# Seven products instead of four double ones in two more pairs, two sets of accumulators, and a new order of work, in an attention and two-MLP kernel

## The chip, the cores and the metric

The kernel runs on one core of one Trainium2 chip. The metric is the device time of one execution in microseconds (us), the median of several runs.

## What is computed

```python
scores = scale * np.matmul(q, k.transpose(0, 1, 3, 2))          # q, k, v: 4 x 8 x 576 x 64
thresh = np.max(scores, axis=-1, keepdims=True) - tau
scores = np.where(scores >= thresh, scores, -1000000000.0)
attn = np.exp(scores - np.max(scores, axis=-1, keepdims=True))
attn = attn / (np.sum(attn, axis=-1, keepdims=True) + 1e-09)
x = np.matmul(attn, v)                                           # as 2304 tokens x 512
h = x @ w_in1                                                    # 512 x 2048
x = (np.maximum(h, 0.0) + alpha * np.minimum(h, 0.0)) @ w_out1   # 2048 x 512
h = x @ w_in2
out = (h - np.tanh(h)) @ w_out2
```

The four weight matrices arrive as 64-bit floats and are made into 32-bit ones on the chip.

## The kernel before

The 2304 tokens are taken in 9 blocks of 256, and each MLP goes through them as blocks 0 to 8 (first MLP) and 9 to 17 (second). Most products are done in split form: an operand is kept as a rounded high part and the remainder (low part), and one product is three matmuls, low with high, high with high, high with low.

**Order of the work.** Nothing loops at run time. Every step is given to `Plan.add` with the engines that may do it, a cost for each, a rank and what it reads and writes; `Plan.order` then simulates the engines and issues, on the engine that can begin first, the ready step with the lowest rank. The constants above the class (`PA`, `OFF`, `POOL_PEN` and so on) are the ranks and penalties. So a change of ranks moves steps on all engines, and can give a copy or a subtraction to another engine. TensorE has 140 filler steps of two matmuls (line 1211) with the last rank, done where nothing else is ready; attention, the first MLP and the preparation of weights run interleaved until attention ends.

**Second MLP.** The 2048 hidden rows of a block are 8 pairs of 2 x 128. For pair n of block m:
- `h_pair` (line 961): 24 matmuls of 256 columns into one PSUM bank. In the second MLP they go to `hp` and to `pt` by turns (line 965), each one bank. ScalarE then takes tanh from that bank (line 987) and VectorE subtracts it (line 994) into `mr`. Only after that may the bank be written again.
- `g` is made from `mr`. With Strassen's algorithm (`STRASSEN`, line 37: pairs 0, 2, 3, 4, 5, 6) VectorE forms four sums `gs` of 128 columns (line 1033), and the seven 128-column operands are split into high and low parts in two pieces (384 and 512 columns).
- `out_products` (line 1069): a Strassen pair adds seven products of 256 columns, 21 matmuls, into seven half banks of `sc` (line 1084). Pairs 1 and 7 are plain: four products of 512 columns, 12 matmuls, into two banks (line 1091).
- After pair 7 the sums of the half banks are formed on VectorE (line 1117) and stored. There is one set of accumulators, the four banks of `sc`, which attention used before.

`out_pair` (line 398) prepares a pair's weights: two loads, `rebias`, `three`, `ends_` and `middle` to make 32-bit floats, and for a Strassen pair four differences (line 430), copies to high parts and subtractions to low parts (line 290). `home` says whose memory it takes: weights of the first MLP that are done with, or what attention leaves.

On TensorE the order in the second MLP is, with few exceptions, the 24 matmuls of one pair, then the output products of the pair before it.

Of the kernel before, what the change touches and what calls it, by code (L numbers as in the profile page):

```python
# [22 lines left out]
P = 128  # L23
BLK = 256
# [23 lines left out]
POOL_PEN = 0.3611  # L50
ACT_PEN = 0.1795
# [6 lines left out]
XR = 18.318  # L58
# [18 lines left out]
class Plan:  # L77
# [38 lines left out]
    def order(self):  # L116
# [42 lines left out]
        late_pen = {"ACT": 0.1, "DVE": 0.0, "POOL": 0.8}  # L159
# [74 lines left out]
def attention_mlp_mlp(ctx: ExitStack, tc: tile.TileContext, kv, q0, q1, tau, w1i, w1o, alpha, w2i, w2o, out):  # L234
# [84 lines left out]
    def turned_float(l, kind, qd, c, rank):  # L319
# [45 lines left out]
        add(any_of(0.56, 0.59, 0.62), rank, three, reads=[raw], writes=[(*raw, 0)], late=l)  # L365
# [22 lines left out]

    def home(p):

        if p < 2:
# [3 lines left out]
        kind, qd = {2: ("o", 0), 4: ("o", 1), 6: ("o", 2), 3: ("i", 3), 5: ("o", 3)}[p]  # L395
        return (lambda: wpool), [f"{kind}{part}{qd}" for part in ("hi", "lo")], [f"{kind}{qd}"]

    def out_pair(p, rank):
# [33 lines left out]
        parts = []  # L432
        if strassen:
            for n_ in range(4):
                add({"DVE": 0.33, "POOL": 0.6}, rank, lambda e, n_=n_: combine(e, n_), reads=t + [(*tk[0], 0)] * (n_ == 1) + [(*tk[0], 1), (*tk[1], 0)] * (n_ == 3),
                    writes=[(*tk[n_ // 2], n_ % 2)], takes=[("o", tk[n_ // 2])] if n_ % 2 == 0 else [], late=True)
            parts = [(lambda: f(0, 0), 0, BLK, [t[0]]), (lambda: f(1), BLK, 3 * BLK, [t[1]]),
                     (lambda: T[tk[0]], 3 * BLK, 5 * BLK, [(*tk[0], 0), (*tk[0], 1)]),
                     (lambda: T[tk[1]], 5 * BLK, 7 * BLK, [(*tk[1], 0), (*tk[1], 1)])]
        else:  # L440
            parts = [(lambda: f(0), 0, 2 * BLK, [t[0]]), (lambda: f(1), 2 * BLK, 4 * BLK, [t[1]])]
        for n_, (x, a, b, r) in enumerate(parts):
            begins = [dst] + ([ROOM] if p < 2 else []) if n_ == 0 else []
            m = (b - a) / 512
            add(any_of(0.1 + 0.42 * m, 0.065 + 0.27 * m, 0.07 + 0.52 * m), rank, lambda e, x=x, a=a, b=b, n_=n_: hi(e, x, a, b, not n_),
                reads=r + ([dst] if n_ else []), writes=[(*dst, n_, 0), *begins], takes=[(x_, dst) for x_ in bufs] if n_ == 0 else [], late=True)
            add(either(0.06 + 0.54 * m, 0.05 + 1.18 * m), rank, lambda e, x=x, a=a, b=b: lo(e, x, a, b), reads=r + [(*dst, n_, 0)], writes=[(*dst, n_, 1)], late=True)
# [32 lines left out]
    def prep(v, rank):  # L480
# [133 lines left out]
    def softmax(tile, n, slots, rank):  # L614
# [346 lines left out]
    def h_pair(p, rank):  # L961
# [3 lines left out]
        hq = hps[l * (p % 2)]  # L965
        hpk, hb = ("hp", l * (p % 2)), [("hp", l * (p % 2))]
# [43 lines left out]
        if not l or p % NPAIR not in STRASSEN:  # L1010
# [55 lines left out]
    def two_banks(k):  # L1066
        return sc[k // 2][:, k % 2 * 512:(k % 2 + 1) * 512]

    def out_products(p, rank):
        m, n = p // NPAIR, p % NPAIR  # L1070
        w, g = ("wp", n), ("g", p)
        strassen = n in STRASSEN

        seven = [(0, 0, 1), (2, 1, 2), (1, 6, 4), (3, 3, 5), (4, 4, 6), (5, 5, 7), (6, 2, 3)]
        begun_banks = set()

        def emit_seven(e, now):
# [30 lines left out]
        def bank(number):  # L1108
            return half_bank(number)[0]
# [219 lines left out]
```

## Time and profile before

| | us |
|---|---|
| median of 3 runs | 1153.53 (1153.4 to 1154.03) |
| the profiled execution | 1156.25 |
| its span, first to last instruction | 1154.5 |
| TensorE busy | 1126.2, 98% of the span |
| VectorE busy | 919.6, 80% |
| ScalarE busy | 640.6, 55% |
| GpSimd busy | 214.4, 19% |

In the rows PE is TensorE's matmul side and PEld its weight loads, DVE is VectorE, ACT is ScalarE, POOL is GpSimd. The profile's times are from one execution. A row of the timeline merges neighbours of one kind: its length runs to the end of the last one, and since matmuls overlap, the distance between two starts is what a group costs. The VectorE rows overlap a little too, so the same holds there.

### The profile page before, as it was taken

Reading aid. Unit: us, or ns where it says so; the run is one execution under the profiler, and the core shown is the slowest. Engines: PE = TensorE matmul, PEld = TensorE weight load, DVE = VectorE, ACT = ScalarE, POOL = GpSimd, SP = SyncE. Lnnn points to the kernel's source line nnn. Section 1 sums busy time; section 2 is a strip of 40 time slices with the busy share of each in tenths; the row PEclk is TensorE's granted clock in tenths of the full one; section 3 lists DMA queues with packets and bytes.
Section 4 is the critical chain, followed back from the end, with each engine's and each line's share of the span. In section 5 each row is a group of like instructions: output and inputs, shape, how many; then the busy total and the mean of one; then the engine's idle time right before and its main releaser. Section 6 shows DMA issues by size and latency. Waiting matters only on the chain.

```text
span 1154.5 us, 23027 instructions
## 1 busy us (share of the span) xinstructions
PE 1126.2 (98%) x8889; PEld 1065.3 (92%) x8889; DVE 919.6 (80%) x2093; ACT 640.6 (55%) x1237; POOL 214.4 (19%) x215
## 2 busy tenths in 40 slices
PE   7999999999999999999999999998999999999998
PEld 6778877999999999999889999997999999999997
DVE  4998897999999998989999797999565565565554
ACT  4777776767667667667676554665223323322322
POOL 0333121232423413214223110010000000000000
PEclk9999999999999999999999999999999999999999
DMA  6654542312123202222112164441110010010000
GB/s 163 186 163 144 166 147 79 89 30 70 49 69 104 70 12 82 70 79 79 46 48 64 27 208 127 157 150 52 37 37 11 28 37 11 28 37 11 10 19 20
DMA packets 55822, 87.10 MB, mean 75 GB/s; under 512 B 18592, under 2 KB 33952, under 8 KB 55712
## 3 DMA queue, kind: packets, MB, share of 16 engines
q1 hardware_dynamic: 55712, 85.62, 24.5%
q8 instruction: 70, 1.15, 0.4%
q14 instruction: 40, 0.33, 0.1%
HBM read 75.64 MB, written 9.96 MB: 74 GB/s over the span
## 4 chain that ended last, share of the span: by engine, by line
PE 79%; DVE 12%; ACT 4%; DMA 2%; issue 2%; POOL 1%; SPq 0%; ACTq 0%; DVEq 0%; POOLq 0%
PE hp L975 21%; PE acc L1162 14%; PE sc L1084 10%; PE pt L975 8%; PE pt L691 4%; PE sc L1091 4%; PE sc L765 3%; PE sc L796 3%; PE acc L1211 2%; PE sc L788 2%; DVE eT L290 2%; DVE e L641 2%; PE sc L757 2%; PE sc L886 2%; DVE st L629 1%
## 5 line engine op out<-in xcount | busy, mean ns | idle before, releaser
L975 PE MATMUL hp<-x,ihi 128*128 128x256 f32 x1728 | 323.0, 285 | 0.5 <-DVE mr L996 0.5
L975 PEld LDWEIGHTS hp<-x,ihi 128*128 128x128 f32 x1728 | 265.3, 189 | 1.4 <-DVE mr L996 0.7
L975 PE MATMUL hp<-x,ilo 128*128 128x256 f32 x864 | 242.8, 281 | 0.0
L1162 PE MATMUL acc<-g,ohi 128*128 128x256 f32 x1152 | 217.2, 286 | 0.4 <-ACT o L285 0.4
L1162 PEld LDWEIGHTS acc<-g,ohi 128*128 128x128 f32 x1152 | 176.6, 189 | 1.4 <-issue 0.7
L975 PEld LDWEIGHTS hp<-x,ilo 128*128 128x128 f32 x864 | 162.9, 189 | 0.0
L1162 PE MATMUL acc<-g,olo 128*128 128x256 f32 x576 | 161.9, 281 | 0.0
L1084 PE MATMUL sc<-wp,g 128*128 128x256 f32 x1134 | 143.3, 280 | 3.9 <-DVE g L290 1.8
L1084 PEld LDWEIGHTS sc<-wp,g 128*128 128x128 f32 x1134 | 137.2, 188 | 5.3 <-DVE g L290 2.2
L641 DVE SCALAR_TENSOR_TENSOR e<-sc,st,e 128x576 f32<-128x576 f32 x144 | 115.4, 814 | 17.7 <-ACT e L637 8.3
L637 ACT ACTIVATE e<-sc,st 128x576 f32<-128x576 f32 x144 | 105.1, 740 | 26.7 <-DVE st L629 16.2
L629 DVE TENSOR_REDUCE st<-sc 128x1 f32<-128x576 f32 x144 | 105.6, 751 | 15.3 <-PE sc L757 8.1
L1162 PEld LDWEIGHTS acc<-g,olo 128*128 128x128 f32 x576 | 108.5, 188 | 0.0
L975 PE MATMUL pt<-x,ihi 128*128 128x256 f32 x576 | 104.1, 281 | 0.0
L285 ACT ACTIVATE eT<-pt 128x512 fp32r<-128x512 f32 (+1 forms) x144 | 85.6, 594 | 22.1 <-PE pt L691 19.9
L691 PE MATMUL pt<-ident,e 128*128 128x128 f32 x576 | 88.1, 275 | 8.6 <-ACT eT L285 4.0
L975 PEld LDWEIGHTS pt<-x,ihi 128*128 128x128 f32 x576 | 89.7, 189 | 1.4
L285 ACT ACTIVATE g<-mr 128x384 fp32r<-128x384 f32 (+1 forms) x98 | 56.3, 574 | 52.5 <-DVE mr L994 36.4
L975 PE MATMUL pt<-x,ilo 128*128 128x256 f32 x288 | 81.0, 281 | 0.0
L290 POOL TENSOR_TENSOR x<-rw,x 128x1024 fp32r<-128x1024 f32 x7 | 20.0, 2855 | 327.2 <-ACT x L285 236.7
L994 DVE TENSOR_TENSOR mr<-hp,mr 128x512 f32<-128x512 f32 x36 | 24.9, 692 | 68.9 <-ACT mr L987 68.9
L691 PEld LDWEIGHTS pt<-ident,e 128*128 128x128 f32 x576 | 65.4, 140 | 15.2 <-ACT eT L285 4.4
(127 smaller groups left out, 2091.7 us busy)
## 6 DMA issues: line engine op xcount, KB each, us to landing
rkv<-in_kv_dram SPq DMA_DIRECT2D x38, 288.0 KB, 2.8
rw<-in_w1i_dram SPq DMA_DIRECT2D x16, 512.0 KB, 4.6
rw<-in_w1o_dram SPq DMA_DIRECT2D x16, 512.0 KB, 4.3
rw<-in_w2i_dram SPq DMA_DIRECT2D x16, 512.0 KB, 4.3
rw<-in_w2o_dram SPq DMA_DIRECT2D x16, 512.0 KB, 4.4
rkv<-in_kv_dram SPq DMA_DIRECT2D x39, 160.0 KB, 2.9
ks<-in_kv_dram SPq DMA_DIRECT2D x18, 288.0 KB, 3.0
x1d<-o SPq DMA_DIRECT2D x18, 256.0 KB, 2.1
```

Source lines behind the costliest of these rows:

```text
L285: e.activation(out=out_, in_=in_, func=AF.Copy, **({} if scale is None else {"scale": scale}))
L290: e.tensor_tensor(out=out_, in0=in_, in1=hi.bitcast(F32), op=ALU.subtract)
L629: e.tensor_reduce(out=T[st][:, 0, j:j + 1], in_=x(s), axis=AX.X, op=ALU.max, negate=True)
L637: e.activation(out=weights(j), in_=x(s), func=AF.Exp, bias=T[st][:, 0, j:j + 1], scale=1.0)
L641: e.scalar_tensor_tensor(out=w_, in0=x(s), scalar=T[st][:, 1, j:j + 1], in1=w_, op0=ALU.is_ge, op1=ALU.mult, accum_out=T[st][:, 2, j:j + 1])
L691: e.transpose(pt[:, c, :], x[:, c * P:(c + 1) * P], ident)
L765: e.matmul(sc[j][:, 192:192 + S][:, c], lhsT=T["qs", v][:, part, j * P:(j + 1) * P], rhs=T["ks", k][:, (1 - j) * D:][:, c], start=(part == ...
L796: e.matmul(po, lhsT=vf[:, c], rhs=T[g][part][:, c, :], start=(c + part == 0), stop=False)
L975: e.matmul(hq[:, k, :], lhsT=weight(l, "i", part, f // 4)[:, c, (f % 4) * P:(f % 4 + 1) * P], rhs=T[f"x{x}", m][:, c, :], start=(n0 + n == ...
L1084: e.matmul(out_, lhsT=x[:, a], rhs=y[:, b], start=(n == 0 and i == 0 and number in (1, 2, 5, 4)), stop=(n == NPAIR - 1 and i == 2), skip_g ...
L1091: e.matmul(two_banks(3 - 2 * t), lhsT=x, rhs=y, start=False, stop=(n == NPAIR - 1 and k == 1 and i == 2), skip_group_check=True)
L1162: e.matmul(acc[t][:, (c % 2) * BLK:(c % 2 + 1) * BLK], lhsT=w[:, c * P:(c + 1) * P], rhs=g[:, k, :], start=(f == 0 and n == 0 and c % 2 == ...
```

## The change

It makes pairs 1 and 7 Strassen pairs. Their weights need 7 x 256 columns instead of 4 x 256, so `beside` puts the last pieces of pairs 6 and 7 into the free eighth of other pairs' tiles. Even and odd blocks get different accumulators: even ones `sc` as before, odd ones the two banks `acc`, the bank `pt` and, for product 4, the other half of `sc`'s last bank. So `h_pair` has only `hp`. Product 4 becomes a half-bank sum of its own at the block's end. Blocks 9 and 10 are taken side by side: pair 0 of both, pair 1 of both, and so on. The ranks, penalties and `RAW` (which scores are done unsplit) are new.

```diff
-STRASSEN = (0, 2, 3, 4, 5, 6)
-PA, PB = 272.298, 4.647
+PA, PB = 363.69, 1.658
-RAW = 20
+RAW = 18
-POOL_PEN = 0.3611
-ACT_PEN = 0.1795
+POOL_PEN = 0.2975
+ACT_PEN = 0
+LPOOL_PEN = 0.0058
+LACT_PEN = 0
...
-        late_pen = {"ACT": 0.1, "DVE": 0.0, "POOL": 0.8}
+        late_pen = {"ACT": LACT_PEN, "DVE": 0.0, "POOL": LPOOL_PEN}
...
+    def beside(p, b):
+
+        return ("wp", p if p < 6 or b < 4 else (b - 3 if p == 6 else b if b < 6 else 8))
...
-        hq = hps[l * (p % 2)]
-        hpk, hb = ("hp", l * (p % 2)), [("hp", l * (p % 2))]
+        hq, hpk, hb = hp, ("hp", 0), [("hp", 0)]
...
-        if not l or p % NPAIR not in STRASSEN:
+        if not l:
...
-    def half_bank(n):
-        k = {1: 0, 6: 1, 2: 2, 3: 3, 7: 4, 5: 5, 4: 6, 8: 7}[n]
-        return sc[k // 4][:, k % 4 * BLK:(k % 4 + 1) * BLK], k // 2
+    def bank_of(m, n):
+
+        if (m - NBLK) % 2 == 0 or n == 3:
+            return sc[n // 2][:, n % 2 * 512:(n % 2 + 1) * 512], ("c", n)
+        if n == 2:
+            return pt.rearrange("p c s -> p (c s)"), ("hp", 1)
+        return acc[n], ("acc", n)
+
+    def half_bank(m, n):
+        k = {1: 0, 6: 1, 2: 2, 3: 3, 7: 4, 5: 5, 4: 6 + (m - NBLK) % 2}[n]
+        x, key = bank_of(m, k // 2)
+        return x[:, k % 2 * BLK:(k % 2 + 1) * BLK], key
...
-        seven = [(0, 0, 1), (2, 1, 2), (1, 6, 4), (3, 3, 5), (4, 4, 6), (5, 5, 7), (6, 2, 3)]
+        seven = [(0, 0, 1), (4, 4, 6), (5, 5, 7), (3, 3, 5), (2, 1, 2), (6, 2, 3), (1, 6, 4)]
...
+        add({"DVE": 0.6}, r, lambda e: total(e, T[o[1]], bank_of(m, 1)[0], T[o[1]]), [keys[1], *oa, *ob], oa + ob, [keys[1]])
+        add({"DVE": 0.35}, r, lambda e: total(e, c(), bank(4), c()), [keys[3], *oc, *od], oc, [keys[3]])
...
+    first, two = NBLK * NPAIR, 2 * NPAIR
+    pairs = [*range(first), *(first + n // 2 + n % 2 * NPAIR for n in range(two)), *range(first + two, NP)]
```

What moves is shown at three places. The first is TensorE at the very end, where the output products of pair 7 of the last block begin (`wp` are weights, `g` values, `sc` the accumulators; x2 is two matmuls). Before, behind the last two products of pair 6:

```order
L1084 MATMUL sc_90<-wp_9841,g 128x256 x2
L1084 MATMUL sc_90<-wp_9842,g 128x256
L1084 MATMUL sc_89<-wp_9841,g 128x256 x2
L1084 MATMUL sc_89<-wp_9842,g 128x256
L1091 MATMUL sc_89<-wp_10200,g 128x512 x2
L1091 MATMUL sc_89<-wp_10201,g 128x512
```

Now, behind the first product of pair 7:

```order
L1101 MATMUL sc_89<-wp_10387,g 128x256 x2
L1101 MATMUL sc_89<-wp_10388,g 128x256
L1101 MATMUL sc_90<-tw,g 128x256 x3
L1101 MATMUL sc_89<-wp_9936,g 128x256 x2
L1101 MATMUL sc_89<-wp_9937,g 128x256
L1101 MATMUL sc_90<-wp_10075,g 128x256 x2
L1101 MATMUL sc_90<-wp_10076,g 128x256
L1101 MATMUL sc_90<-wp_10387,g 128x256 x2
L1101 MATMUL sc_90<-wp_10388,g 128x256
```

Twelve matmuls of 512 columns, of which the first three stand here, are now 21 of 256, some with weights that lie beside those of other pairs (`tw`, `wp_9936`, `wp_10075`).

The second is VectorE while the second MLP begins, the last rows ahead of the sixth subtraction of tanh (`mr`); `rw` and `tw` are weights being made into floats, `o` their differences, `wp` their low parts. Before:

```order
L290 TENSOR_TENSOR wp_10013<-o,wp_10012 128x512
L354 SCALAR_TENSOR_TENSOR rw<-rw 128x512
L290 TENSOR_TENSOR wp_10013<-o,wp_10012 128x512
L359 SCALAR_TENSOR_TENSOR tw<-tw,rw 128x512
L354 SCALAR_TENSOR_TENSOR rw<-rw 128x512 x2
L359 SCALAR_TENSOR_TENSOR tw<-tw,rw 128x512
L290 TENSOR_TENSOR wp_10091<-tw,wp_10090 128x256
L430 TENSOR_TENSOR o<-tw 128x256
L290 TENSOR_TENSOR g<-mr,g 128x384
L290 TENSOR_TENSOR g<-gs,g 128x512
L430 TENSOR_TENSOR o<-tw,o 128x256
L994 TENSOR_TENSOR mr<-pt,mr 128x512
```

Now:

```order
L350 SCALAR_TENSOR_TENSOR rw<-rw 128x512
L1046 TENSOR_TENSOR gs<-mr 128x128
L355 SCALAR_TENSOR_TENSOR tw<-tw,rw 128x512
L1046 TENSOR_TENSOR gs<-gs,mr 128x128
L1046 TENSOR_TENSOR gs<-mr 128x128
L1046 TENSOR_TENSOR gs<-mr,gs 128x128
L286 TENSOR_TENSOR g<-mr,g 128x384
L350 SCALAR_TENSOR_TENSOR rw<-rw 128x512
L286 TENSOR_TENSOR g<-gs,g 128x512
L355 SCALAR_TENSOR_TENSOR tw<-tw,rw 128x512
L286 TENSOR_TENSOR wp_10076<-tw,wp_10075 128x256
L1007 TENSOR_TENSOR mr<-hp,mr 128x512
```

The same kinds of work stand there; before, 24 rows lie between the fifth and the sixth subtraction, and now 11, those ahead of the last one.

The third is VectorE where a later block ends and the next begins (`o` are now the output sums), up to the second subtraction of the new block. Before:

```order
L1117 TENSOR_TENSOR o<-sc_89,o 128x256
L1117 TENSOR_TENSOR o<-sc_90,o 128x256 x3
L994 TENSOR_TENSOR mr<-hp,mr 128x512
L1117 TENSOR_TENSOR o<-sc_89,o 128x512
L1033 TENSOR_TENSOR gs<-mr 128x128
L290 TENSOR_TENSOR g<-mr,g 128x384
L1033 TENSOR_TENSOR gs<-gs,mr 128x128
L1033 TENSOR_TENSOR gs<-mr 128x128
L1033 TENSOR_TENSOR gs<-mr,gs 128x128
L1117 TENSOR_TENSOR o<-sc_90,o 128x512
L290 TENSOR_TENSOR g<-gs,g 128x512
L994 TENSOR_TENSOR mr<-pt,mr 128x512
```

Now:

```order
L1124 TENSOR_TENSOR o<-acc_91,o 128x256
L1046 TENSOR_TENSOR gs<-mr 128x128
L1124 TENSOR_TENSOR o<-pt,o 128x256
L1046 TENSOR_TENSOR gs<-gs,mr 128x128
L1046 TENSOR_TENSOR gs<-mr 128x128
L1046 TENSOR_TENSOR gs<-mr,gs 128x128
L286 TENSOR_TENSOR g<-mr,g 128x384
L283 TENSOR_SCALAR g<-gs 128x512
L1124 TENSOR_TENSOR o<-pt,o 128x256 x2
L1124 TENSOR_TENSOR o<-acc_92,o 128x512
L1124 TENSOR_TENSOR o<-sc_90,o 128x256
L1007 TENSOR_TENSOR mr<-hp,mr 128x512
```

The six sums lay on both sides of a subtraction and are now all ahead of one; the low part of `g`'s second piece (`g<-gs,g`), in the row ahead of the last before, is GpSimd's now.

## Rows read from the trace of the kernel before

**Rows 1.** The page's busy times, shares of the span and instructions by engine

```profile
PE 1126.2 (98%) x8889; PEld 1065.3 (92%) x8889; DVE 919.6 (80%) x2093; ACT 640.6 (55%) x1237; POOL 214.4 (19%) x215
```

**Rows 2.** Windows of 40 us: length, busy time and count by engine, granted clock, DMA

```profile
0.00:40.00 40.00, 34.15 (x213) 26.99 (x215) 22.73 (x55) 20.26 (x40) 4.71 (x12) 0.96 0.60 165
680.00:720.00 40.00, 40.00 (x340) 40.00 (x340) 33.26 (x62) 19.77 (x34) 1.77 (x2) 1.00 0.39 117
...
760.00:800.00 40.00, 36.75 (x290) 35.26 (x290) 38.84 (x89) 23.98 (x43) 0.00 (x0) 1.00 0.38 119
800.00:840.00 40.00, 38.67 (x297) 36.52 (x296) 23.73 (x56) 12.43 (x21) 0.00 (x0) 1.00 0.08 27
840.00:880.00 40.00, 40.00 (x319) 39.00 (x318) 23.32 (x48) 11.26 (x20) 2.45 (x1) 1.00 0.08 27
1080.00:1120.00 40.00, 40.00 (x319) 39.02 (x318) 22.82 (x54) 11.53 (x20) 0.00 (x0) 1.00 0.04 14
```

**Rows 3.** TensorE's waits from 700 us on: for whom, total, times, longest

```profile
PE sc L1084 <- DVE g L290: 1.8, 1, 1.8
PE sc L1084 <- DVE wp L290: 1.5, 2, 1.2
PE sc L1091 <- DVE o L1117: 0.9, 1, 0.9
```

**Rows 4.** Timeline of TensorE around a Strassen and a plain pair: start, length, instructions

```profile
885.03 2.61 PE L1084 MATMUL sc<-wp,g 128*128 128x256 f32 x21
887.48 0.39 PE L975 MATMUL hp<-x,ihi 128*128 128x256 f32 x2
...
890.34 2.91 PE L1091 MATMUL sc<-wp,g 128*128 128x512 f32 x12
893.09 0.40 PE L975 MATMUL pt<-x,ihi 128*128 128x256 f32 x2
```

**Rows 5.** Timeline, all engines: from a pair's last input matmul to its `g`

```profile
1122.09 2.61 PE L1084 MATMUL sc<-wp,g 128*128 128x256 f32 x21
1122.29 0.60 ACT L987 ACTIVATE mr<-pt 128x512 f32<-128x512 f32 x1 [2.53 <-PE pt L975]
1122.92 0.69 DVE L994 TENSOR_TENSOR mr<-pt,mr 128x512 f32<-128x512 f32 x1 [2.43 <-ACT mr L987]
...
1124.54 0.40 PE L975 MATMUL hp<-x,ihi 128*128 128x256 f32 x2
1124.58 0.55 DVE L290 TENSOR_TENSOR g<-mr,g 128x384 fp32r<-128x384 f32 x1
...
1125.37 0.69 DVE L290 TENSOR_TENSOR g<-gs,g 128x512 fp32r<-128x512 f32 x1 [0.23 <-ACT g L285]
```

**Rows 6.** Timeline of VectorE, instructions that follow each other without a wait

```profile
774.38 0.28 DVE L1033 TENSOR_TENSOR gs<-mr,gs 128x128 f32<-128x128 f32 x1
774.58 0.55 DVE L290 TENSOR_TENSOR g<-mr,g 128x384 fp32r<-128x384 f32 x1
775.05 0.42 DVE L287 TENSOR_SCALAR g<-gs 128x512 fp32r<-128x512 f32 x1
775.39 0.69 DVE L354 SCALAR_TENSOR_TENSOR rw<-rw 128x512 int32<-128x512 int32 x1
775.99 0.69 DVE L290 TENSOR_TENSOR g<-gs,g 128x512 fp32r<-128x512 f32 x1
```

**Rows 7.** Timeline of a stretch in attention, VectorE and GpSimd at the same time

```profile
603.63 0.88 POOL L290 TENSOR_TENSOR vs<-rkv,vs 128x320 fp32r<-128x320 f32 x1 [0.25 <-ACT vs L285]
...
603.80 1.26 DVE L290 TENSOR_TENSOR g<-mr,g 128x512 fp32r<-128x512 f32 x1
```

**Rows 8.** Timeline of the program's end, TensorE and VectorE

```profile
1143.23 2.61 PE L1084 MATMUL sc<-wp,g 128*128 128x256 f32 x21
...
1146.30 1.67 DVE L1117 TENSOR_TENSOR o<-sc,o 128x256 f32<-128x256 f32 x4 [0.36 <-ACT o L285]
1146.78 3.04 PE L1091 MATMUL sc<-wp,g 128*128 128x512 f32 x12 [0.93 <-DVE o L1117]
...
1149.86 0.69 DVE L1117 TENSOR_TENSOR o<-sc,o 128x512 f32<-128x512 f32 x1 [0.69 <-PE sc L1091]
```

More of the change, by code (lines that the diff above doesn't have):

```diff
@@ L364, in turned_float @@
         add(any_of(0.575, 0.335, 0.59), rank, rebias, reads=[raw], writes=[t], takes=[("tw", t)], late=l)
-        add(any_of(0.56, 0.59, 0.62), rank, three, reads=[raw], writes=[(*raw, 0)], late=l)
+        add(any_of(0.565, 0.345, 0.62), rank, three, reads=[raw], writes=[(*raw, 0)], late=l)
         add({"DVE": 0.64}, rank, ends_, reads=[raw, (*raw, 0)], writes=[(*raw, 0)])
@@ L430, in combine @@
             e.tensor_tensor(out=tt(n), in0=x, in1=y, op=ALU.subtract)
[L432 to L447, printed above, removed]
+        for n_ in range(4):
+            add({"DVE": 0.33, "POOL": 0.6}, rank, lambda e, n_=n_: combine(e, n_), reads=t + [(*tk[0], 0)] * (n_ == 1) + [(*tk[0], 1), (*tk[1], 0)] * (n_ == 3),
+                writes=[(*tk[n_ // 2], n_ % 2)], takes=[("o", tk[n_ // 2])] if n_ % 2 == 0 else [], late=True)
@@ new lines, in out_pair @@
+        parts = [(lambda: f(0, 0), 0, 1, [t[0]]), (lambda: f(1), 1, 3, [t[1]])]
+        for k in range(0, 4, 1 if p > 5 else 2):
+            m = 1 if p > 5 else 2
+            parts.append((lambda k=k, m=m: tt(k, m), 3 + k, 3 + k + m, [(*tk[x // 2], x % 2) for x in range(k, k + m)]))
+        for x, a, b, r in parts:
+            begins = [dst] + ([ROOM] if p in (0, 6) else []) if not a else []
+            m, host = (b - a) / 2, beside(p, a)
+            takes = [(x_, dst) for x_ in bufs] if not a else [("tw", host)] if host == ("wp", 8) else []
+            add(any_of(0.1 + 0.42 * m, 0.065 + 0.27 * m, 0.07 + 0.52 * m), rank, lambda e, x=x, a=a, b=b: hi(e, x, a, b),
+                reads=r + ([dst] if a else []) + ([host] if host not in (dst, ("wp", 8)) else []),
+                writes=[(*dst, a, 0), *begins] + ([(*host, 0)] if host == ("wp", 8) else []), takes=takes, late=True)
+            add(either(0.06 + 0.54 * m, 0.05 + 1.18 * m), rank, lambda e, x=x, a=a, b=b: lo(e, x, a, b),
+                reads=r + [(*dst, a, 0)], writes=[(*dst, a, 1)] + ([(*host, 1)] if host == ("wp", 8) else []), late=True)
@@ L452, in attention_mlp_mlp, with parts_of @@
+    def parts_of(p):
+        return [(*("wp", p), a, part) for a in ((0, 1, 3, 4, 5, 6) if p > 5 else (0, 1, 3, 5)) for part in range(2)]
     visits, unit = [], []
@@ L1077, in emit_seven @@
         def emit_seven(e, now):
-            gh, gl = T[g], T["gl", p]
-            wh, wl = T[w]
             for a, b, number in now:
-                a, b = slice(a * P, (a + 1) * P), slice(b * BLK, (b + 1) * BLK)
-                out_, bank = half_bank(number)
+                a = slice(a * P, (a + 1) * P)
+                gh, gl = T[g][:, a], T["gl", p][:, a]
+                wh, wl = (operand(n, part, b, b + 1) for part in range(2))
+                out_, bank = half_bank(m, number)
                 for i, (x, y) in enumerate(((gl, wh), (gh, wh), (gh, wl))):
-                    e.matmul(out_, lhsT=x[:, a], rhs=y[:, b], start=(n == 0 and i == 0 and number in (1, 2, 5, 4)),
+                    e.matmul(out_, lhsT=x, rhs=y, start=(n == 0 and i == 0 and number in ((1, 7, 2) if m == NBLK + 1 else (1, 7, 2, 4))),
@@ L1104, in out_products @@
+        for now in (seven[:1], seven[1:2], seven[2:4], seven[4:6], seven[6:]):
+            halves = sorted({half_bank(m, x[2])[1] for x in now})
+            a_s = {int(x[0] > 2) for x in now}
+            add({"PE": 0.355 * len(now)}, rank + MLP_PE, lambda e, now=now: emit_seven(e, now),
+                [*parts_of(n), *[(*g, x) for x in a_s], *[("gl", p, x) for x in a_s]], halves, halves)
         if n < NPAIR - 1:
@@ L1108, in bank @@
         def bank(number):
-            return half_bank(number)[0]
+            return half_bank(m, number)[0]
+        keys = [bank_of(m, x)[1] for x in range(4)]
         def p1(e):
```

115 lines of the change are left out of this document (48 added, 67 removed).

## The prediction

> **What bounds the kernel now.** Read first the page's busy line [rows 1]: TensorE is busy 98% of the span, 28.3 us of 1154.5 are idle, and no other engine comes near. Then the windows [rows 2]: from 840 us on TensorE has no idle time at all, and VectorE, at 23 of 40 us, no pressure on it. So the second MLP is as long as its matmuls. Where the 28.3 us lie: 5.9 before 40 us, 4.6 in the two windows from 760 us, 0.9 in the wait ahead of the last plain pair and 4.7 behind its last matmul [rows 8], which leaves 12.2 over the whole of attention. The granted clock is at its upper level (2.4 GHz) everywhere but at the start. The third view, TensorE's waits [rows 3], says what it waits for from 760 us on: low parts of `g` and of the weights `wp`, which VectorE makes, 38.84 of 40 us busy there. So three things are worth money: matmul time, the entry to the second MLP, and the waits in attention.
>
> All terms are differences in the profiled execution (1156.25, its span 1154.5 and 1.75 around it); the median of the runs is 2.72 lower, and I take the sum from the median. About 2.3 us (0.2%) is what a measurement can tell.
>
> **Products.** A Strassen pair starts at 885.03 and the next group at 887.48: 2.45 us for 21 matmuls. A plain pair takes from 890.34 to 893.09: 2.75 us for 12, or 0.229 each [rows 4]. Each of the 18 plain pairs that becomes a Strassen pair gives back 0.30 us where TensorE is the bound. The very last lies on the tail, below: 17 x 0.30 = **-5.1 us**. Both forms run in this kernel at this clock, so the bounds are narrow, -4.5 to -5.5.
> A rule of the Trainium skill speaks against this term: "TensorE: Matmul & The Clock Gate", section Back-to-back issue gap, gives for a sustained stream 131 ns at 512 columns and 81 at 128. By it a plain pair would be 12 x 131 = 1.57 us and a Strassen pair at least 21 x 81 = 1.70, an estimate from that page, and the swap would cost 18 x 0.13 = 2.3 us instead of gaining. The trace disagrees, with 229 ns at 512 columns, and the measurement decides.
>
> What a Strassen pair costs elsewhere: four sums at 0.20, low parts at 0.47 and 0.60, the tanh subtraction at 0.60, 2.5 us of VectorE by distances between starts [rows 6], under the 5.3 us of TensorE that one pair takes (2.45 + 24 x 0.1176, the latter being 40 us / 340 matmuls [rows 2]). It is hidden, also where a plain pair needed less.
>
> **One input bank instead of two.** The next pair's first input matmul now waits for the tanh subtraction. In the chain of one pair [rows 5] output products start at 1122.09, tanh at 1122.29, the subtraction ends at 1123.61, and the next input matmul starts at 1124.54. It fits with 0.93 us to spare, so I cost it at **0**. The cover is the 2.45 us of the other pair's output products; VectorE or ScalarE late by more than 0.93 us is paid in full, pair by pair.
>
> **Entry to the second MLP.** Two full windows hold 2 x 319 matmuls; those from 760 us hold 290 + 297 [rows 2]. 51 are missing: 51 x 40 / 319 = 6.4 us lost, 3.3 of it shown as the waits for `g` and `wp` [rows 3]. The order says why. Between the first and the eighth tanh subtraction of this MLP VectorE has 48 instructions 512 wide at 0.60, 24 of 128 at 0.20, 15 of 256 at 0.34, 6 of 384 at 0.47 and 9 copies at 0.34 or less [rows 6] (256 lies on the line through the others): 44.4 us. TensorE has 300 matmuls at 0.1176 and 12 at 0.229: 38.0 us. VectorE is 6.4 behind, the time lost. Afterwards the weights are used for two blocks, so the same preparation has twice the time. In the new order the lag is largest at the seventh subtraction: 40 x 0.60 + 24 x 0.20 + 12 x 0.34 + 6 x 0.47 + one of 1024 at 1.14 + a copy = 37.2 us against 297 x 0.1176 = 34.9, so 2.3 behind. It then shrinks, to 0.8 at the tenth. I take 2.4 lost instead of 6.4: **-4.0 us**. Bounds: all of it goes (-6.4), or GpSimd's new share spoils it (+4.5, rival 2). The nearest evidence is that the same count hit today's loss, so I stay near -4.
>
> **Block ends.** Today they cost nothing [rows 2]. Now all six sums (0.60 and five at 0.34, one bank each), the subtraction, four sums for `g`, a 0.47 and a 0.34 stand in one gap: 4.5 us, under 5.3. But `g`'s first low part comes behind sums, and the second goes to GpSimd, for which I take 1.4 us (0.88 for 320 columns [rows 7], times 512 / 320). From the start T of the last products: subtraction done at T+1.5, sums and first low part by T+3.9, high copy T+4.4, GpSimd T+6.0. The next output products start at T+5.3 and need it from their second product, T+5.65. 0.35 late at each of seven block ends, 2.5 us at most; the planner fills part of it with input matmuls, and its bound below is 0. I take **+1.0**. With two sets of accumulators the sums themselves hold nobody up; the shared last bank is asked for 2.1 us into the next block's first pair, at T+7.4, and its sum is done by about T+6.4.
>
> **Tail.** Today from the end H of the last input matmuls (1143.23) to the end of the last sum (1150.55) it is 7.3 us [rows 8]. Now pair 7 needs a Strassen `g`: 3.97 us behind H as in [rows 5], against 2.45 of cover. Product 1 goes at about H+3.1, the other six end at H+6.2. The sums are a chain of six on VectorE: product 6 at H+4.4, ScalarE's copy to H+5.0, four sums at 0.42 (four take 1.67 [rows 8]) to H+6.7, 0.69 and 0.42 to H+7.8. **+0.5 us**; it lies between 0 and +1.
>
> **Attention.** The new ranks move work: by the order, VectorE loses 17 us of its 609 up to the last softmax (12 normalisations, 6 low parts of k, copies), ScalarE gains 14, GpSimd 30 over the program (counts by mean durations). TensorE's work there is the same but for 12 matmuls done later. Its 12.2 us of idle time are short waits in a chain of four engines; less VectorE work shortens some, slower GpSimd lengthens others. I take **0**, with -6 (half of the waits go) and +6 (half as many again) as bounds.
>
> Sum: -5.1 + 0 - 4.0 + 1.0 + 0.5 + 0 = -7.6. 1153.5 - 7.6 = **1145.9 us**.
>
> **Rivals.**
> 1. *The single bank paces the second MLP* (the other side). Place: the first input matmul of each of 72 pairs, waiting for the subtraction. It decides as soon as the subtraction is on average later than 0.93 us. At 1.13 late, 72 x 0.2 = 14.4 us: 1160.3. For it: ScalarE and VectorE now serve block ends, x loads and `g` in one file. Against: half of VectorE's time there is free [rows 2]. 5%.
> 2. *The entry is not eased.* GpSimd takes some 15 of the conversions there, where it did nothing between 760 and 840 us [rows 2]. A VectorE subtraction of 512 columns that met a GpSimd one took 1.26 instead of 0.69 us [rows 7]. If half of the 15 meet one, 7 x 0.57 = 4 more, and nothing is gained: 1149.9, 14%. If all do, 8.6 more: the lag is 10.9 and the sum +0.9: 1154.4, 4%. The Trainium skill, "SBUF — State Buffer", section Who interferes with whom, says that a VectorE instruction with two SBUF inputs contends with a GpSimd one that reads SBUF; these two rows agree.
> 3. *Attention gains*: fewer waits, 1139.9, 14%. *Attention loses*: 1151.9, 10%. For the first: 17 us less of 609 on VectorE. Against: ScalarE and GpSimd carry it in the same chain.
> 4. *The swap gives nothing*: were a 512-column matmul 0.204 us (2.45 / 12) or less. 17 x 0 + the rest: 1151.0. Rows 4 speak against it: 1%. The clock page's rule above is this rival.
>
> **How the numbers follow.** The forecast has 52%, at 1143 to 1149. Faster by over 2.3 us is all below 1151.2: 52 + 14 + 14 + 1 and a third of the 10, 0.84. Within: the rest of the 10 and the 4, 0.11. Slower: rival 1, 0.05. The range goes to the attention cases, 1140 to 1152, and leaves out the far ends of both, rival 1 and the worst of rival 2, about 2 in 10.
>
> **What would show it.** Products: every group of output products starts 2.45 us before the next group, none 2.75. Entry: at least 625 matmuls in the two 40 us behind the first output products, VectorE busy over 90% for some 55 us, waits for `wp` under 1 us. Single bank: no wait of an input matmul for the subtraction in steady state. Block ends: waits for `g` from GpSimd, 0.2 or so each. Tail: a wait for `g` of 0.6 and one of 0.6. I am wrong if input matmuls wait for `mr` in most pairs, or if idle time before 700 us differs by more than 6.

## The result and the profile after

The change made the kernel slower: the median of six runs is 1159.96 us, before in the same comparison 1153.47 us, ratio 1.0053 (95% interval 1.003 to 1.0076). One of the six, 6088.66 us, was disturbed and is not in the ratio; the other five have a median of 1158.83. The profiled execution took 1158.83 us, 2.6 more than that of before.

The page's busy line of the changed kernel answers to [rows 1]:

```profile
PE 1121.8 (97%) x9051; PEld 1072.2 (93%) x9051; DVE 918.8 (79%) x2136; ACT 669.9 (58%) x1298; POOL 254.9 (22%) x249
```

TensorE is busy 4.4 us less and idle 6.9 us more. Where, the windows tell (columns as in [rows 2]):

```profile
720.00:760.00 40.00, 38.02 (x318) 37.61 (x317) 38.53 (x75) 30.16 (x54) 7.32 (x6) 1.00 0.55 179
760.00:800.00 40.00, 40.00 (x342) 40.00 (x342) 39.85 (x96) 27.02 (x53) 13.53 (x7) 1.00 0.27 87
800.00:840.00 40.00, 38.37 (x322) 37.96 (x321) 25.45 (x61) 14.71 (x25) 2.81 (x2) 1.00 0.04 15
840.00:880.00 40.00, 39.10 (x329) 38.70 (x328) 23.78 (x59) 13.01 (x24) 0.00 (x0) 1.00 0.08 27
1080.00:1120.00 40.00, 40.00 (x341) 40.00 (x340) 23.70 (x61) 13.96 (x25) 1.30 (x1) 1.00 0.04 14
```

The window from 760 to 800 us is full now, but the second MLP begins 7 us earlier (its first input matmul at 738.09 us, before at 745.37), and part of the entry's idle time lies in the window ahead, which was full before. The steady second MLP, from 840 us on, where before had no idle time at all, is full only in the last window shown. The view of TensorE's waits from 700 us on (for whom, total, times, longest) names the loss:

```profile
PE sc L1101 <- DVE o L1124: 12.2, 9, 1.9
PE hp L988 <- DVE mr L1007: 2.5, 3, 1.4
PE sc L1101 <- DVE g L286: 1.0, 2, 0.5
```

Output products wait nine times for VectorE's output sums. The timeline of all engines at such a place, the end of block 11 (start, length, instructions, idle time before them and who ended it). Even and odd count from the second MLP's first block, so `sc` serves blocks 9, 11, 13, 15 and 17:

```profile
877.26 2.33 PE L1101 MATMUL sc<-wp,g 128*128 128x256 f32 x18
...
879.68 0.42 DVE L1124 TENSOR_TENSOR o<-sc,o 128x256 f32<-128x256 f32 x1 [0.90 <-PE sc L1101]
...
880.23 0.42 DVE L1124 TENSOR_TENSOR o<-sc,o 128x256 f32<-128x256 f32 x1
...
880.36 2.39 POOL L286 TENSOR_TENSOR x<-rw,x 128x1024 fp32r<-128x1024 f32 x1 [47.15 <-ACT x L281]
880.56 2.34 DVE L1046 TENSOR_TENSOR gs<-gs,mr 128x128 f32<-128x128 f32 x1
...
880.70 0.62 PE L1101 MATMUL sc<-tw,g 128*128 128x256 f32 x3 [1.10 <-DVE o L1124]
...
884.03 1.80 DVE L1124 TENSOR_TENSOR o<-sc,o 128x256 f32<-128x256 f32 x4
...
885.88 0.62 PE L1101 MATMUL sc<-wp,g 128*128 128x256 f32 x3 [1.33 <-DVE o L1124]
```

Three things stand there. Product 4 of the old block (`tw`) waits 1.10 us, although no sum reads its bank yet: the one at 880.23 reads the other bank of the same two-bank tile (product 7's; product 4 adds to the last bank). VectorE's 128-column sum at 880.56 takes 2.34 us instead of 0.28, for as long as GpSimd's subtraction of the next `x` runs. And product 4 of the new block, which the planner put second in its pair, waits 1.33 us for the four sums that are late by it. The end of block 12 shows the same lateness on another instruction, a copy that takes 0.42 elsewhere:

```profile
926.15 2.61 POOL L286 TENSOR_TENSOR x<-rw,x 128x1024 fp32r<-128x1024 f32 x1 [40.61 <-ACT x L281]
926.41 2.63 DVE L283 TENSOR_SCALAR g<-gs 128x512 fp32r<-128x512 f32 x1
...
930.82 0.62 PE L1101 MATMUL sc<-wp,g 128*128 128x256 f32 x3 [1.87 <-DVE o L1124]
```

The last block end, near 1105 us, has no next `x` to make, and there TensorE does not wait at all: the window from 1080 us above is full.

One wait costs more than itself. Behind another wait of 1.87 us, at 1021.53, the granted clock fell to 0.50, the lower of its two levels (1.2 GHz), as windows of 2 us show:

```profile
1020.00:1022.00 2.00, 0.47 (x3) 0.44 (x3) 1.97 (x5) 0.00 (x0) 1.19 (x1) 0.97 0.00 0
1022.00:1024.00 2.00, 2.00 (x11) 1.88 (x9) 1.49 (x6) 0.52 (x1) 0.00 (x0) 0.50 1.00 318
1024.00:1026.00 2.00, 2.00 (x14) 2.00 (x13) 0.00 (x0) 0.00 (x0) 0.00 (x0) 0.68 0.61 207
1026.00:1028.00 2.00, 2.00 (x19) 2.00 (x18) 1.16 (x2) 0.00 (x0) 0.00 (x0) 1.00 0.00 0
```

The price can be read off: the same 24 matmuls (3 of product 4, 6 input, 15 output) take from 930.82 to 934.02, 3.20 us, where the clock stayed, and from 1021.53 to 1026.12, 4.59 us, here. A fall costs 1.4 us.

The tail, timeline of TensorE, VectorE and SP's store issues:

```profile
1143.04 2.66 PE L1101 MATMUL sc<-wp,g 128*128 128x256 f32 x21
...
1147.05 2.06 PE L1101 MATMUL sc<-wp,g 128*128 128x256 f32 x15
...
1149.21 2.73 DVE L1124 TENSOR_TENSOR o<-sc,o 128x256 f32<-128x256 f32 x6 [2.21 <-PE sc L1101]
1151.67 2.46 SPq L1145 DMA_DIRECT2D out_dram<-o  x4
```

All six sums start behind the last product, and all four stores behind the fifth sum, which ends at 1151.61.

### The profile page after: what moved, and what is told of

The parts are those of the page before. It is cut to its first block, busy times and chain, and to the rows that moved or that the text cites. A ratio compares the mean times of both kernels' runs of the same rounds, so it can differ in the third digit from the quotient of the medians.

```text
span 1157.0 us, 23558 instructions
## 1 busy us (share of the span) xinstructions
PE 1121.8 (97%) x9051; PEld 1072.2 (93%) x9051; DVE 918.8 (79%) x2136; ACT 669.9 (58%) x1298; POOL 254.9 (22%) x249
## 3 DMA queue, kind: packets, MB, share of 16 engines
q8 instruction: 71, 1.16, 0.4%
## 4 chain that ended last, share of the span: by engine, by line
PE 80%; DVE 11%; ACT 4%; DMA 2%; issue 2%; SPq 0%; POOL 0%; DVEq 0%; ACTq 0%; POOLq 0%
PE hp L988 30%; PE acc L1164 14%; PE sc L1101 9%; PE pt L705 4%; PE acc L1101 4%; PE sc L779 4%; PE sc L810 3%; PE sc L802 2%; PE acc L1213 2%; PE pt L1101 2%; PE acc L802 1%; PE sc L900 1%; DVE eT L286 1%; DVE e L655 1%; PE sc L771 1%
## 5 line engine op out<-in xcount | busy, mean ns | idle before, releaser
L988 PE MATMUL hp<-x,ihi 128*128 128x256 f32 x2304 | 428.3, 285 | 2.5 <-DVE mr L1007 2.5
L988 PEld LDWEIGHTS hp<-x,ihi 128*128 128x128 f32 x2304 | 354.6, 190 | 4.8 <-DVE mr L1007 4.0
L988 PE MATMUL hp<-x,ilo 128*128 128x256 f32 x1152 | 324.7, 282 | 0.0
L988 PEld LDWEIGHTS hp<-x,ilo 128*128 128x128 f32 x1152 | 218.1, 189 | 0.0
L1007 DVE TENSOR_TENSOR mr<-hp,mr 128x512 f32<-128x512 f32 x72 | 49.7, 691 | 110.5 <-ACT mr L1000 110.4
L1000 ACT ACTIVATE mr<-hp 128x512 f32<-128x512 f32 x72 | 43.0, 597 | 163.1 <-PE hp L988 159.0
L655 DVE SCALAR_TENSOR_TENSOR e<-sc,st,e 128x576 f32<-128x576 f32 x144 | 115.1, 814 | 12.9 <-ACT e L651 6.3
L1101 PEld LDWEIGHTS sc<-wp,g 128*128 128x128 f32 x909 | 113.3, 190 | 10.2 <-DVE o L1124 8.7
L286 DVE TENSOR_TENSOR g<-mr,g 128x384 fp32r<-128x384 f32 (+1 forms) x118 | 74.4, 630 | 13.2 <-ACT g L281 5.3
L281 ACT ACTIVATE e<-e,st 128x576 f32<-128x576 f32 x82 | 62.7, 770 | 25.4 <-DVE st L663 25.0
L1009 DVE SCALAR_TENSOR_TENSOR mr<-mr,nalpha,hp 128x256 f32<-128x256 f32 x144 | 64.8, 474 | 12.9 <-ACT mr L1002 12.0
```

Source lines behind the costliest of these rows:

```text
L281: e.activation(out=out_, in_=in_, func=AF.Copy, **({} if scale is None else {"scale": scale}))
L286: e.tensor_tensor(out=out_, in0=in_, in1=hi.bitcast(F32), op=ALU.subtract)
L655: e.scalar_tensor_tensor(out=w_, in0=x(s), scalar=T[st][:, 1, j:j + 1], in1=w_, op0=ALU.is_ge, op1=ALU.mult, accum_out=T[st][:, 2, j:j + 1])
L988: e.matmul(hq[:, k, :], lhsT=weight(l, "i", part, f // 4)[:, c, (f % 4) * P:(f % 4 + 1) * P], rhs=T[f"x{x}", m][:, c, :], start=(n0 + n == ...
L1007: e.tensor_tensor(out=T[r], in0=hq, in1=T[r], op=ALU.subtract)
L1009: e.scalar_tensor_tensor(out=T[r][:, k, :], in0=T[r][:, k, :], scalar=nalpha[:, f0 + k:f0 + k + 1], in1=hq[:, k, :], op0=ALU.mult, op1=ALU ...
```

## The experiments

Theories: A, a tile of two banks makes a product wait for a sum in the other bank (and the reverse). C, GpSimd's subtraction of `x` holds VectorE up at block ends; rival D, product 4 simply comes too early in the shared bank. G, the new ranks alone do what attention gained. The other letters are explained in the expectations where they come up.

**One-bank tiles.** `sc` is released when attention is done, and four tiles of one bank take its place; no engine's order changes.

```diff
+            spool.release()
+            fpool = ctx.enter_context(tc.tile_pool(name="fpool", bufs=1, space=PSUM))
+            four.extend(fpool.tile([P, 512], F32, name=f"so{k}") for k in range(4))
```

> Only change: the four banks of sc become four tiles of one bank each once attention is done; every engine's order stays as it is. Theory A (the waits go by tiles, and a tile of two banks makes a product wait for a sum that reads the other bank): the four waits of 1.1 us ahead of the tw products at 830, 881, 971 and 1064 us vanish, the row of PE sc waiting for DVE o falls from 12.2 us to 7.7, in 5 waits, and the run is 3 to 5 us faster than the changed kernel (about 1155). Rival B (the product really waits for its own bank): the row stays at 12.2 us, and the time at 1160.

1155.46 us, ratio to before 1.0005 (0.9996 to 1.0015). The waits in that profile:

```profile
PE so L1110 <- DVE o L1133: 9.4, 5, 1.9
```

The four waits of 1.1 us are gone, and A is shown. The total fell by 2.8 instead of 4.5: after blocks 11, 13 and 15 TensorE is now 1.1 us earlier, and the wait for the late sums is 1.87 there instead of 1.33. About 1 us of the gain is the tail, below.

**x later.** ScalarE's and GpSimd's halves of making the next `x` go some two pairs later in the emitted order, for blocks 13 to 17:

```diff
+            x = [o for o in order if o[0] in T["made", m]]
+            order = [o for o in order if o not in x]
+            at = [o[0] for o in order].index(T["low", (m - 1) * NPAIR + 2]) + 1
+            order[at:at] = x
```

> Only change: the high and low parts of the next x (ScalarE's copy and GpSimd's subtraction, 128x1024) of blocks 13 to 17 are issued two pairs later; nothing moves on TensorE and VectorE. Theory C (GpSimd's 2.4 us subtraction meets VectorE's work at a block's end, so that a sum or a copy takes 2.3 to 2.6 us instead of 0.3 to 0.4): the waits of 1.33 us (886, 977, 1069) and 1.87 us (931, 1022) shrink to under 0.3 each, the row of PE sc waiting for DVE o falls from 12.2 to about 4.5 us, and the run is 7 to 9 us faster than the changed kernel, more if the clock falls less often (about 1152). Rival D (product 4 comes too early in a bank that it shares with the old block's product 4, whatever GpSimd does): those five waits stay above 1 us each and the time within 2 us of 1160.

1153.19 us, ratio 0.9988 (0.9975 to 1.0001):

```profile
PE hp L988 <- DVE mr L1007: 6.1, 8, 1.8
PE sc L1101 <- DVE o L1124: 4.4, 4, 1.1
```

C is shown: the five waits for sums are gone, VectorE's 128-column sums at block ends are back at 0.28 us. But five waits of 0.70 us for `mr` came up at the same block ends, so some 6 us were won instead of 7 to 9.

**Product 4 last.**

```diff
-                [*parts_of(n), *[(*g, x) for x in a_s], *[("gl", p, x) for x in a_s]], halves, halves)
+                [*parts_of(n), *[(*g, x) for x in a_s], *[("gl", p, x) for x in a_s]], halves, halves, after=range(len(plan.ops) - 4, len(plan.ops)) if now == seven[6:] and n == 0 and m > NBLK + 1 else ())
```

> Only change: in the first pair of blocks 11 to 17 product 4, which stands in the bank shared with the old block, goes behind the pair's other six products on TensorE; no other engine's order changes. If D holds, the five waits of 1.33 and 1.87 us vanish and nothing takes their place: the row of PE sc waiting for DVE o at 4.5 us, the time about 1152. If C holds, VectorE is still late by 2 us there, and part of the wait comes back at the next thing it owes TensorE (low parts of g, or mr ahead of the next input products): I expect 2 to 4 us of waits under other names, and about 1154.

1164.09 us, ratio 1.0083 (1.007 to 1.0096), slower:

```profile
PE hp L988 <- DVE mr L1007: 13.2, 8, 2.5
PE sc L1101 <- DVE o L1124: 4.4, 4, 1.1
```

D falls: with product 4 out of the way TensorE runs into the single input bank instead, and waits there longer, 10.7 us under the other name instead of my 2 to 4. The clock fell three times in this profile (behind waits of 2.47, 1.94 and 1.94 us), once in the changed kernel's, the program's start and end left aside.

**Both edits.** One-bank tiles and x later.

> The edits of the first two runs together. If A and C hold, TensorE waits for output sums under 1 us in all, its idle time behind 840 us falls from 12 us to under 1.5 up to the tail, and the time is 12 us below the changed kernel's 1160, or some 14 if its falls of the clock go too: 1146 to 1149, 4 to 7 us faster than the kernel before. If the loss is another (the single bank hp, or the clock alone), the time stays above 1153.

1146.77 us, ratio 0.9932 (0.9917 to 0.9947), as expected. The 0.70 waits remain; the timeline at the start of block 15 shows what they are:

```profile
1012.60 0.88 PE L1110 MATMUL so<-wp,g 128*128 128x256 f32 x6
1012.79 0.60 ACT L1002 ACTIVATE mr<-hp 128x512 f32<-128x512 f32 x1 [3.50 <-PE hp L990]
...
1013.42 0.69 DVE L1009 TENSOR_TENSOR mr<-hp,mr 128x512 f32<-128x512 f32 x1 [0.70 <-ACT mr L1002]
...
1014.17 0.51 PE L990 MATMUL hp<-x,ihi 128*128 128x256 f32 x2 [0.70 <-DVE mr L1009]
```

Six output matmuls, then input matmuls of the next pair, while tanh and subtraction have only begun.

**A third edit, input matmuls behind.** The six input matmuls at those ends go behind all seven products:

```diff
+            h = [o for o in order[a:b] if o[1] == "PE" and not end - 5 <= o[0] < end]
+            order = order[:a] + [o for o in order[a:b + 1] if o not in h] + h + order[b + 1:]
```

> The two edits that worked (one-bank tiles, x later) and a third: at the ends of blocks 12 to 17 the six input matmuls that stood between the first two output products and the other five go behind all seven. Theory E (with those six matmuls of the next pair ahead, hp has only 0.7 us of output products as cover instead of 2.45, and waits 0.70 us for mr at five block ends): the five waits of 0.70 us vanish, the row of PE hp waiting for DVE mr falls from 6.3 us to 2.8, and the time from 1146.8 to about 1143.3. Rival F (the products then wait for the low part of g, which GpSimd makes): the five waits stay under another name, and the time at 1146 to 1147.

1140.35 us, ratio 0.9875 (0.9858 to 0.9891), 3 us better than expected and 6.4 below the run with two edits (the profiled execution, 1144.17, is the slowest of four):

```profile
PE hp L990 <- DVE mr L1009: 2.6, 3, 1.7
PE so L1110 <- DVE g L288: 1.0, 2, 0.5
```

E is shown. From 880 to 1120 us TensorE has no idle time. From start to start of the matmuls each of the five waits of 0.70 us had cost 0.97, 4.8 together; the other 1.6 us are not traced.

**The order of TensorE alone**, product 4 last and the input matmuls behind, with `x` and the tiles as the change has them:

> The changed kernel (two-bank tiles, x made at the block's end as it was) with the order of TensorE alone changed: in the first pair of blocks 11 to 17 product 4 last, as in the run that did only this, and at the ends of blocks 12 to 17 also the six input matmuls of the next pair behind all seven products. If E is right that those six matmuls turned the late VectorE into a wait for mr, the wait for mr falls from 13.2 us to 2.5 plus at most 0.5 at five ends, the row of PE sc waiting for DVE o stays at 4.4, and the time is 1153 to 1155: GpSimd's subtraction is then covered by the order alone. If VectorE is simply too late whatever the order, waits for mr of 1 us or more stay at five block ends, and the time above 1157.

1154.89 us, ratio 1.0009 (0.9996 to 1.0021):

```profile
PE sc L1101 <- POOL g L286: 3.2, 2, 1.6
PE acc L1101 <- POOL g L286: 3.2, 3, 1.1
```

The waits for `mr` went, as E says; but behind its subtraction of `x` GpSimd makes the low part of `g`, and is late with that, five waits of 1.05 to 1.59 us. So the time is in the range that I gave, but with waits that I had not expected: the order covers part of the lateness, not all.

**The low part of x on VectorE**, with one-bank tiles, at its place at the block's end:

```diff
+                e = "DVE" if i in [T["x lo", m] for m in range(NBLK + 4, 2 * NBLK)] else e
```

> The one-bank tiles, and the low part of the next x at the same place of the order, but on VectorE instead of GpSimd (1.2 us in line, between the output sums). By theory C GpSimd's 2.4 us subtraction cost VectorE 2.0 to 2.2 us each time, so this costs it 0.9 to 1.0 less: the five waits of 1.87 us for DVE o (9.4 us) shrink to 0.8 to 1.0 each, 4 to 5 us in all, and the time from 1155.5 to about 1150. If VectorE was late for another reason, it is now later still: waits of 2.5 us or more each, and slower than 1156.

1155.44 us, ratio 1.0014 (1.0003 to 1.0024), and the five waits are still 1.87 or 1.88 us each. My number missed (about 1150): on VectorE the subtraction met GpSimd's other piece of work, the low part of `g`, and took 2.29 us instead of the 1.22 of other places:

```profile
924.87 1.29 POOL L288 TENSOR_TENSOR g<-gs,g 128x512 fp32r<-128x512 f32 x1 [43.65 <-DVE g L285]
924.95 2.29 DVE L288 TENSOR_TENSOR x<-rw,x 128x1024 fp32r<-128x1024 f32 x1
```

It started 0.08 us behind GpSimd's and ended 1.08 us behind GpSimd's end. In line it costs VectorE 2.29 us, where the copy that met GpSimd in the run with one-bank tiles had lost 2.21 (2.63 instead of 0.42); so the waits stay the same. That is C's mechanism with the roles changed, not its refutation.

**One set of accumulators.** All blocks in `sc`, two input banks by turns, blocks 9 and 10 one after the other:

```diff
-        if (m - NBLK) % 2 == 0 or n == 3:
+        if True:
...
-        hq, hpk, hb = hp, ("hp", 0), [("hp", 0)]
+        hq, hpk, hb = (hp, pt.rearrange("p (k c) s -> p k (c s)", k=2))[l * (p % 2)], ("hp", l * (p % 2)), [("hp", l * (p % 2))]
```

> The changed kernel without two of its parts: one set of accumulators for all blocks (the four banks of sc), two input banks by turns as before, blocks 9 and 10 one after the other; Strassen pairs for all eight and the new ranks stay. By my terms: ranks -6.4, products -5.1, entry not eased (6 to 7 us of waits between 740 and 840 us), block ends without waits as before: 1153.5 - 11.5 + 1 = 1143. Rival I (two sets are needed once all pairs are Strassen pairs, since the next block's first products want the banks 2 us after the last ones): waits for output sums at seven block ends of 1 us or more, and 1150 or above.

1172.61 us, ratio 1.0159 (1.0144 to 1.0174), 30 us above my 1143. Rival I's waits are there, 18.6 us for sums, and at the entry waits for `mr` of up to 3.29 us. With the two edits:

> The kernel with one set of accumulators (1172.6 us) with the two edits, one-bank tiles and x later. It had waits of 1.11 and 1.36 us for output sums at seven block ends. By A the 1.11 vanish. By C the 1.36 shrink. If both go to under 0.3, the second set of accumulators is not needed for the block ends, and the time is 1172.6 - 17 = 1155, of which 9 us is the entry; if the 1.36 stay or grow at all seven (rival I), about 1164.

1155.4 us, ratio 1.0009 (1.0 to 1.0019): of the waits for sums one of 1.16 us is left, at 846 us, and 0.57 for `g` at five ends. So rival I, that one set cannot do, held only while `sc` had two-bank tiles and `x` stood at the block's end; these two edits take away 17.2 of the 18.5 us lost against before, the falls of the clock that the waits brought among them. What remains is the entry, 6.6 us of waits for `mr`.

**Not side by side.** The two edits, with blocks 9 and 10 one after the other:

```diff
-    pairs = [*range(first), *(first + n // 2 + n % 2 * NPAIR for n in range(two)), *range(first + two, NP)]
+    pairs = [*range(NP)]
```

> The kernel with the two edits (one-bank tiles, x later), with blocks 9 and 10 one after the other instead of side by side. By my entry term (-4.0) it is 4 us slower than with them side by side: 1150.8, with about 6 us of waits for g, wp and mr between 740 and 800 us against 2.8. Rival J (side by side only moves the preparation's waits): within 1.5 us of 1146.8.

1159.87 us, ratio 1.0046 (1.003 to 1.0062), 13 us slower than side by side where I had 4. Of its nine waits for `mr`, 12.9 us in all, four at the entry make 9.7 us (side by side three, 2.8); the other five are those at the block ends, of 0.70 us or less. 30.33 of the 40 us from 760 us are busy, and the clock fell twice, at 795 and 850 us. With eight Strassen pairs more weights have to be ready early, and a single bank passes the lateness on: blocks in file under the new ranks have no wait for `mr` with six Strassen pairs (the next run), 6.6 us with eight and two input banks (the run before this one), 9.7 with eight and one.

**The ranks alone.** The kernel before with the change's constants and costs; TensorE's order up to the second MLP, and every engine's up to 680 us, is that of the changed kernel.

```diff
-PA, PB = 272.298, 4.647
+PA, PB = 363.69, 1.658
...
```

> The kernel before with nothing changed but the ranks, penalties, costs and RAW of the change; up to the second MLP every engine's order is that of the changed kernel, behind it the second MLP of before. Theory G (attention's gain is the ranks' alone): TensorE's idle time up to 720 us is 11 to 13 us, as in the changed kernel, instead of 18; the entry still loses some 6 us; the time is 6 us below before's, 1148. Rival H (the gain needs the changed second MLP behind it): no faster than 1152.

1139.73 us, ratio 0.9877 (0.9858 to 0.9896): 14 us faster than before, more than twice what I expected, and some 20 us faster than the whole change. Its busy line, two windows and the one row in the view of TensorE's waits from 700 us on:

```profile
PE 1120.2 (99%) x8889; PEld 1064.4 (94%) x8889; DVE 903.1 (79%) x2042; ACT 655.5 (58%) x1268; POOL 241.7 (21%) x241
40.00:720.00 680.00, 673.86 (x5395) 635.43 (x5395) 611.45 (x1423) 484.32 (x968) 203.67 (x209) 1.00 0.31 93
760.00:800.00 40.00, 39.78 (x315) 38.59 (x314) 34.83 (x78) 20.20 (x37) 7.34 (x5) 1.00 0.26 86
PE sc L1093 <- DVE o L1119: 1.2, 2, 0.9
```

G is shown, for the constants and costs together; which of them does it was not tried. Up to 720 us 5 + 6.1 = 11.1 us are idle instead of 18.1. And the entry's loss is gone too, without any part of the new second MLP: the first tanh subtraction is at 741.35 us instead of 752.68, and by the order and my durations VectorE has 41.1 us of work between the first and the eighth instead of 44.4.

## Why the prediction was wrong

Profiled execution against profiled execution:

| step | predicted | measured as idle time | measured from start to start | from |
|---|---|---|---|---|
| Products | -5.1 | -5.1 | -4.9, with the last pair | every steady pair 2.45 us, none 2.75 |
| One input bank | 0 | 0 in steady state | 0 | no wait for `mr` outside entry and block ends |
| Entry | -4.0 | -3.4 | -2.9 | 3.0 us of waits instead of 6.4 lost |
| Block ends | +1.0 | +12.2, and 1.4 for a fall of the clock | +17.6 | nine waits |
| Tail | +0.5 | +2.7 | +2.9 | 13.96 us from the last input matmul to the end, before 11.27 |
| Attention | 0 | -6.4 | -10.1 | idle up to 720 us 11.7 instead of 18.1 |

Measured as idle time the parts sum to +1.4, but the two executions differ by 2.6. Idle time is not all that a wait takes: the view counts it only from the end of the last matmul, and the first matmuls behind it start further apart (0.22 us instead of 0.12 at 880.70). From each matmul's start to the next, less 0.1176 us for 256 columns and 0.229 for 512, the wait of 1.10 us costs 1.38, that of 1.33 costs 1.84 and that of 1.87 costs 2.39; nine waits make 15.8 us, and the fall of the clock 1.4. For attention I take the first input matmul of the second MLP (745.37 and 738.09 us) and add the 72 and 48 matmuls of the first MLP that are still to come. So counted the parts sum to 2.6. Before's profiled execution was 2.7 us above its median, the changed kernel's is at the median of its five, so the medians differ by 5.4, where I had -7.6.

**The step that failed is Block ends**, in its sentences "the sums themselves hold nobody up" and "the shared last bank is asked for 2.1 us into the next block's first pair, at T+7.4, and its sum is done by about T+6.4". From T = 877.26 it was asked for at T+7.3 and came free at T+8.6. The answer came 2.2 us late. The time of the question was right by luck: the new pair began at T+6.8 instead of T+5.3, most of it the wait of 1.10 us ahead of it, and product 4 was asked for 0.5 us into the pair and not 2.1. With `x` later the last bank's sum is done at T+6.6, with one-bank tiles as well at T+5.5. Two reasons lay open before:
- GpSimd's subtraction of the next `x` stands at the block's end in the old order too, and meets a 128-column sum there at six block ends; TensorE did not wait for it. The kernel before, timeline at the end of block 11:

```profile
893.45 2.50 POOL L290 TENSOR_TENSOR x<-rw,x 128x1024 fp32r<-128x1024 f32 x1 [40.54 <-ACT x L285]
893.61 2.49 DVE L1033 TENSOR_TENSOR gs<-mr,gs 128x128 f32<-128x128 f32 x1
```

  I costed meetings at the entry, by one row [rows 7], and none here. I also read a wrong price from that row: 0.57 us was lost to a GpSimd instruction of 0.88 of which 0.71 was left; with 2.19 left of one of 2.39, at 880.56, VectorE loses 2.06, and with 2.34 left, at 893.61, 2.21. In each of these the loss is the rest of GpSimd's instruction less 0.13 or 0.14. The Trainium skill, "SBUF — State Buffer", section Who interferes with whom, calls the shared ports an exclusive lock: who issues first holds them for the whole instruction, and the other blocks. These runs agree (2.34 us beside 2.39, 2.63 beside 2.61, and 2.29 for work of 1.22 beside 1.29). By it, where GpSimd is first, the price is the rest of its instruction, not a factor on VectorE's.
- I took banks for the unit of the waits, as the planner does. They go by tiles. It stood in [rows 8]: the first plain product there waits 0.93 us for a sum in the other bank of its tile. I read that wait as the bank's own.

The single bank was safe where I looked, in a steady pair, and not at block ends: there it has less cover (0.7 us of products where input matmuls were pulled ahead), and a late VectorE is paid there (five waits of 0.70 us with `x` later, 10.7 us with product 4 last), as rival 1 says of its mechanism; its place was wrong.

**Tail.** My sums' end was H+7.8; with one-bank tiles it is H+7.95 (1129.36 to 1137.31 in the run with three edits), in the changed kernel H+8.90, because the first sum waits for all products of the two-bank tile. What I left out is the stores: four issues of 2.46 us on SP, which began 1.3 us before the last sum's end in the old kernel and begin 0.3 us before it now. That is 1.1 us.

**Entry** came out near its size by luck, for half of the reason. The ranks alone bring its loss to nearly nothing with six Strassen pairs; with eight in file its waits for `mr` are 6.6 or 9.7 us, and side by side wins most of that back. I had put the whole gain down to side by side. My 6.4 us lost were also not all preparation: [rows 3] shows three of the view's six lines, and two of the others, waits of 0.6 us for an output sum and of 0.5 for ScalarE's copy of one, stand at the end of block 9 and cost 1.85 us from start to start. So block ends did not cost quite nothing before. Rival 2's price did not come up because the meetings mostly went the other way: at 771.35 and 781.66 us GpSimd's differences took 3.67 and 3.87 us (0.73 at 764.15) beside a VectorE without a gap, and from 738 to 835 us VectorE lost 1.1 us in all.

**Attention** reached my bound, not my value: rival 3. Its idle time fell by 6.4 us, from start to start it is 10.1. I had counted the work moved from VectorE, and did not trust it; the idle time up to 700 us differs by more than the 6 us that I named as a sign of being wrong.

So the change is three: ranks, 14 us gained; Strassen pairs, 5 us gained in TensorE's time; and what was rearranged for these pairs, which at the block ends, the entry and the tail costs all that and more. With three edits of order and tiles the whole stands at 1140.35, as fast as the ranks alone at 1139.73 (the intervals lie on each other), both 1.2% faster than the kernel before. Where the 5 us of products went is argued, not shown: the profiled execution with three edits has 2.6 us of waits at the entry and a fall of the clock, 1.0 us of waits for `g` and 2.0 more of tail, but it lies 5.5 us above that of the ranks alone, where the medians lie 0.6 apart. No run has the eight pairs without these losses.

## What to carry to other kernels

Where a buffer that carried slack is taken away, look for the lateness that the slack hid: list what else runs on every engine at that moment, GpSimd above all, and price a meeting in which GpSimd is first by the rest of its instruction. Split an accumulator into tiles as fine as the waits are meant to be. And when a change moves ranks and structure together, run the ranks alone first: here they alone were as fast as all of it with three edits.

## What the runs showed of the hardware

- A GpSimd instruction that starts first holds VectorE for its rest, less 0.13 or 0.14 us in the meetings named above, even when VectorE's own is a copy of 0.42 us with one input (2.63) or a sum of 128 columns (2.34). Sums that read an accumulator bank ran in their usual time beside it (0.41 and 0.69 us beside GpSimd's 1.26 at 884.28), but at 880.56 they stood in the queue behind the instruction that was held. The other way round, in the kernel before GpSimd's subtraction of `x` took 5.04 us instead of 2.50 at 754.96, while VectorE worked on without a gap, at its usual times, until 758.35.
- The granted clock fell behind some of TensorE's waits and not behind others of the same length: behind 1.87 us at 1021.53 it went to 0.50, behind 1.87 us at 930.82 in the same execution it stayed at 1.00. A fall cost 1.4 us beside the wait. The five times of the changed kernel spread from 1156.69 to 1162.43 us, before's from 1151.35 to 1155.39, and the mean granted clock of each execution goes with its time: 0.998 at 1156.69, 0.995 at 1157.9 and 1158.83, 0.994 at 1161.1 and 1162.43. That fits a differing number of falls; behind which waits they came in the executions without a profile was not seen.
